# Moving the first two of four VectorE folds inside a top-k search: top-k attention followed by an expert layer

## The chip, the cores and the metric

The kernel runs on one core of one Trainium2 chip. The metric is the device time of one execution in microseconds. Engines are named as in the profile: PE is TensorE (PEld its weight loads), DVE is VectorE, ACT is ScalarE, POOL is GpSimd, SP is SyncE, which issues most of the DMAs.

## The reference

The first half is attention that keeps, for each query, the keys with the 32 highest scores. The second half routes each token to one of eight experts.

```python
# q, k, v: (8, 8, 576, 64) float32
scores = q @ k.T / sqrt(64)
kth = np.partition(scores, -32, axis=-1)[..., -32:-31]
scores = np.where(scores >= kth, scores, -1e9)
attn = softmax(scores)                      # + 1e-9 in the divisor
x = (attn @ v) as (8 * 576, 8 * 64)         # tokens x 512
logits = x @ w_gate                         # 8 experts
e = argmax(logits);  gate_w = softmax(logits)[e]
y = gate_w * (relu(x @ w1[e]) @ w2[e])      # 512 -> 1024 -> 512
```

## The kernel before

Work is cut into 144 items, here called slots: 8 batches of 18, each with two tiles of 128 queries against 576 keys. The list `work` holds them, and the function `loop` (L1123) goes through it. Its body writes out one order of instructions for TensorE, ScalarE and VectorE by hand (`tc.manual_schedule`, L1204), and these three engines run it as written. GpSimd's arithmetic keeps its program order too (`in_turn`). In one slot `i`:

- `products` (L292) has TensorE compute scores, and `scores` (L299) has ScalarE copy them from PSUM into a tile `s`. This runs three slots ahead (`AHEAD = 3`).
- `fold` and `fold_on` make the search shorter. With the 576 scores of a query as two halves, `fold` writes the larger of each pair to `h` (L306) and the smaller to `l` (L308). `fold_on` does the same with the halves of `h`: the larger go to `few` (L314), the smaller to `hl` (L316). All four are VectorE operations on two tiles in SBUF.
- `search` (L333) finds the 32nd highest value. It first takes the eight highest of `l` and of the two halves of `hl` into `few` (L345), and then does four rounds on `few`: a scan for the eight highest (L354), and, but for the last round, their replacement (L362), each for both tiles. After round 0 GpSimd computes `nbias` (L358).
- After the search, ScalarE scales the threshold to `low` (L371) and turns the scores into `w` (L387, `depths`); GpSimd subtracts `w` from `s` twice, once for each tile (L396, `less`), and computes `doubt` (L377); ScalarE takes the exponential (L404), TensorE transposes (L415 to L429), ScalarE copies the result out, and TensorE multiplies by the values (L450).

The search has places, called `tick`, after each scan and each replacement of rounds 1 to 3, where one operation of another job may stand on VectorE. These jobs wait in the list `aside`. They are the reciprocal of the divisors `rz` (L479, once per unit of nine tiles, after ScalarE's L472 to L477); once per batch the choice of the expert (L510 to L520) and the places of the rows (L546 to L556); and in six batches the tables of blocks (L611 to L651, over two slots).

GpSimd has more in its queue: products with the divisors for the logits (L487 to L492) and for the rows `x` (L500), the indirect DMAs that scatter the rows (L567), and those that store the output (L808).

The expert blocks (L893, L910) are cut into pieces, and `loop` places a number of them in each slot that it works out from the slot's index. What is left of them after the last slot runs as a tail on TensorE.

The search is called with a function `then`, which stands in front of the last round's scans:

```python
for r in range(R):
    if r == R - 1:
        then()
    for m in m_all:
        nc.vector.max(out=tops[:, m, r * 8:(r + 1) * 8], in_=src[m])
        if r:
            tick()
```

Of the kernel before, what the change touches and what calls it, by code (L numbers as in the profile page):

```python
# [42 lines left out]
def kernel(  # L43
# [216 lines left out]
    def open_unit(n):  # L260
        n.z = k.small.tile([P, NT], F32, name="z")

    def tails(tiles):
        return tiles[0][1] == 2 * NC
# [30 lines left out]
    def scores(got):  # L295

        s = k.att.tile([P, 2, 2, HF], F32, name="s", bufs=2 if k.exact else 4)
        return s, [
            lambda m=m, ps=ps: nc.scalar.copy(s[:, m, :, :], ps[:, :, 0:HF]) for m, ps in enumerate(got)  # L299
        ]  # L300

    def fold(s):

        f = SimpleNamespace()
        f.h = k.att.tile([P, 2, HF], F32, name="h", bufs=1)
        nc.vector.tensor_tensor(f.h, s[:, :, 0, :], s[:, :, 1, :], op=ALU.max)  # L306
        f.l = k.att.tile([P, 2, HF], F32, name="l")
        nc.vector.tensor_tensor(f.l, s[:, :, 0, :], s[:, :, 1, :], op=ALU.min)  # L308
        return f

    def fold_on(f):

        f.few = k.att.tile([P, 2, LW], F32, name="few", bufs=3)
        nc.vector.tensor_tensor(f.few[:, :, 0:QF], f.h[:, :, 0:QF], f.h[:, :, QF:HF], op=ALU.max)  # L314
        f.hl = k.att.tile([P, 2, QF], F32, name="hl", bufs=1)
        nc.vector.tensor_tensor(f.hl, f.h[:, :, 0:QF], f.h[:, :, QF:HF], op=ALU.min)  # L316
# [66 lines left out]
    def depths(s, low):  # L383

        w = k.att.tile([P, 2, S], F32, name="w", bufs=1 if k.exact else 3)
        for m in range(2):
            nc.scalar.activation(  # L387
                w[:, m, :], s[:, m, :, :].rearrange("p j k -> p (j k)"), AF.Relu,
                scale=-STEEP, bias=low[:, m:m + 1],
            )  # L390
        return w

    def less(s, w):

        for m in range(2):
            k.last_pool = in_turn(nc.gpsimd.tensor_tensor(  # L396
                w[:, m, :], s[:, m, :, :].rearrange("p j k -> p (j k)"), w[:, m, :], op=ALU.subtract
            )).ins
# [403 lines left out]
    def evacuate(upto=None):  # L802

        while due and (upto is None or upto in [kind for kind, _ in due]):
            due.pop(0)[1]()
# [131 lines left out]
    with fast:  # L937
# [30 lines left out]
        def put_stores():  # L968
            while stores:
                stores.pop(0)()  # L970
# [6 lines left out]
        def pieces(n):  # L977
            nonlocal current, left
            while n > 0 and left > 0:
                if current is None:  # L980
                    if not landed(loaded[0]):
                        break
                    now = loaded.pop(0)
                    if hasattr(now, "half"):
                        current = long_block(now, following)
                    else:
                        current = block(now, following, stores.append)
                    ahead()
                if clock is None:
                    evacuate()  # L990
                step = next(current)
                if step == "pause":
                    if clock is not None:
                        break
                    continue
                if step == "last":
                    current = None
                n -= 1
                left -= 1
            return n  # L1000

        def scatter(n):
            nonlocal left
            for _ in range(min(n, len(scatters))):
                scatters.pop(0)()
            if not scatters and coming:
                waiting.extend(coming)
                left += len(coming) * PIECES
                coming.clear()
                ahead()  # L1010
# [88 lines left out]
        def at_place(name):  # L1099
            for end in list(late):  # L1100
                if end[1] == name:
                    end[1] = next(end[0], None)
                    if end[1] is None:
                        late.remove(end)

        got_of, s_of, f_of, w_of = {}, {}, {}, {}

        def tiles_of(i):
            b, g = work[i]
            return [(unit[b * U + u], tile) for u, tile in g]  # L1110

        def turning(i):
            return transposed(tiles_of(i), w_of.pop(i))

        def multiply(i):
            tiles = tiles_of(i)
            got_of[i] = products(tiles)
            n, tile = tiles[0]
            more = n.b * U + n.u + 2
            if tile == (NC - 1 if n.u % 2 else 2 * NC) and more < len(units):  # L1120
                unit.append(load_unit(*units[more]))

        def loop():  # L1123
            nonlocal credit, rate, clock
            for i in range(min(AHEAD, len(work))):
                multiply(i)
                s_of[i], steps = scores(got_of.pop(i))
                for step in steps:
                    step()
            multiply(AHEAD)  # L1130
            f_of[0] = fold(s_of[0])
            fold_on(f_of[0])
            for i, (b, g) in enumerate(work):
                tiles = tiles_of(i)
                u, tile = g[0]
                if tile == 0 and u % 2 == 0:
                    open_unit(tiles[0][0])
                if tails(tiles):
                    open_unit(tiles[1][0])

                then = lambda: None
                if i + 1 < len(work):
                    f_of[i + 1] = fold(s_of[i + 1])
                    then = lambda: fold_on(f_of[i + 1])
                low, nbias, doubts = search(tiles, s_of[i], f_of.pop(i), then)
                at_place("small")
                w_of[i] = depths(s_of[i], low)
                less(s_of.pop(i), w_of[i])
                doubts()
                put_stores()  # L1150
                scatter(1)
                at_place("pool")
                at_place("relu")
                at_place("rows")
                at = i % per_batch
                if at == FIRST and b:
                    rate = new_of[b - 1] * PIECES / (U * NT)
                credit += rate * len(g)
                room = left
                if b == B - 1 and at >= ARRIVED:  # L1160
                    room -= KEEP
                    credit = room / (len(work) - i)
                share = {0: 0.5, 1: 1.2, 2: 1.6, 3: 0.5, 2 * NC: 1.4}[tile]
                now = max(0, min(int(credit * share + 0.5), room))
                credit -= now
                clock = i
                if i + AHEAD < len(work):
                    s_of[i + AHEAD], steps = scores(got_of.pop(i + AHEAD))
                    for step in steps:
                        step()  # L1170
                evacuate()
                at_place("turn")
                turns = turning(i - 1) if i else iter(())
                next(turns, None)
                part = min(BETWEEN, now - now // 2)
                rest = pieces(part)
                next(turns, None)
                rest = pieces(now - now // 2 - part + rest)
                weights(tiles, w_of[i], nbias)
                next(turns, None)  # L1180
                evacuate()
                if i + AHEAD + 1 < len(work):
                    multiply(i + AHEAD + 1)
                if tile == NC - 1:
                    end = ending(b, u)
                    late.append([end, next(end)])
                at_place("products")
                at_place("weights")
                credit = min(credit + pieces(now // 2 + rest), 6 * rate)

            for _ in turning(len(work) - 1):
                pass
            assert len(late) == 1
            clock = None
            for place in late[0][0]:
                if place == "rows":
                    pieces(4)
            kept = left - (SURE + HALVES + PLAIN) * PIECES
            assert kept >= 0, kept
            k.apart = True  # L1200
            pieces(kept)

        credit = rate = 0.0
        with tc.manual_schedule(engines={mybir.EngineType.PE, mybir.EngineType.Activation, mybir.EngineType.DVE}):  # L1204
            loop()
# [132 lines left out]
```

## Time and profile before

| | |
|---|---|
| time, median of 3 runs | 1338.02 us (1337.96 to 1338.56) |
| the profiled execution | 1339.03 us |
| its span, first to last instruction | 1337.4 us |
| mean granted TensorE clock | 0.955 |
| busy: PE, DVE, ACT, POOL | 1189.3, 1076.6, 930.8, 661.9 us |
| HBM read, written | 191.42 MB, 21.80 MB |

The page divides the span into 40 slices and gives each engine's busy share in tenths. A group line gives line, engine, operation, tiles and count, then the busy time in us and the mean of one instruction in ns, then the idle time before them and what ended it. A timeline line gives start, duration, engine, line, operation and count; instructions of one kind in a row are merged. A waits line names who waited for whom: total us, times, longest.

### The profile page before, as it was taken

The numbers are of one execution on the slowest core, as the hardware profiler recorded it, in microseconds if no ns is written. First come the engines' busy times: TensorE is split into PE (matmuls) and PEld (weight loads), VectorE is DVE, ScalarE is ACT, GpSimd is POOL, SyncE is SP. The second block draws the span as 40 slices with busy tenths as digits, with TensorE's granted clock in tenths as the row PEclk, the third lists the DMA queues.
The fourth block names the chain that finished last, engine by engine and source line by source line (L and its number), as shares of the span: only waits on it lengthen the run. The fifth ranks groups of instructions, "written<-read, shape, count | busy, mean of one in ns | idle before, by whom it ended". The sixth has DMA issues, their size and how long they took to land. (4 is left out here: it accounts for less than half of the span.)

```text
span 1337.4 us, 24295 instructions
## 1 busy us (share of the span) xinstructions
PE 1189.3 (89%) x7570; PEld 831.4 (62%) x7570; DVE 1076.6 (81%) x4629; ACT 930.8 (70%) x2125; POOL 661.9 (49%) x805
## 2 busy tenths in 40 slices
PE   5667766766799999999999999999999999999995
PEld 3344443444466766676677666666677667699973
DVE  7999999999999999999999999999999932000000
ACT  4788788887888888888787888887778851111110
POOL 3454547555755665567555756475547642000000
PEclk9788788888899999999999999999999999999998
DMA  2000001001384348435855294329452739946790
GB/s 84 30 29 30 30 29 65 29 29 38 122 305 168 108 164 288 160 110 175 297 208 179 74 350 170 118 76 372 171 204 87 283 116 332 369 146 219 290 342 18
DMA packets 95563, 214.36 MB, mean 160 GB/s; under 512 B 4926, under 2 KB 25662, under 8 KB 95424
## 3 DMA queue, kind: packets, MB, share of 16 engines
q1 hardware_dynamic: 88800, 192.45, 40.8%
q0 software_dynamic: 6336, 19.97, 4.2%
q8 instruction: 61, 1.00, 0.3%
q14 instruction: 78, 0.64, 0.2%
q10 hardware_dynamic: 288, 0.30, 0.1%
HBM read 191.42 MB, written 21.80 MB: 159 GB/s over the span
## 5 line engine op out<-in xcount | busy, mean ns | idle before, releaser
L396 POOL TENSOR_TENSOR w<-s,w 128x576 f32<-128x576 f32 x288 | 410.2, 1444 | 418.4 <-ACT w L387 418.4
L893 PE MATMUL ph<-xTs,w 128*128 128x128 f32 x2048 | 250.2, 276 | 5.9 <-ACT xTs L790 5.9
L893 PEld LDWEIGHTS ph<-xTs,w 128*128 128x128 f32 x2048 | 239.1, 192 | 21.9 <-issue 14.6
L910 PE MATMUL py<-w,hT 128*128 128x512 f32 x512 | 236.2, 597 | 0.0
L404 ACT ACTIVATE w<-w,nbias 128x576 f32<-128x576 f32 x288 | 224.1, 792 | 3.0 <-POOL w L396 2.0
L292 PE MATMUL sc<-qkb 64*128 64x288 f32 (+1 forms) x1280 | 206.0, 473 | 9.5 <-ACT s L299 5.1
L387 ACT ACTIVATE w<-s,low 128x576 f32<-128x576 f32 x288 | 207.6, 768 | 4.7
L415 PE MATMUL wTm<-turn,w 128*128 128x128 f32 x1152 | 170.1, 287 | 32.0 <-ACT xl L468 21.4
L415 PEld LDWEIGHTS wTm<-turn,w 128*128 128x128 f32 x1152 | 132.0, 145 | 92.5 <-issue 34.4
L299 ACT COPY s<-sc 128x576 f32<-128x576 f32 x288 | 168.9, 640 | 10.4 <-PE sc L292 10.4
L1217 DVE CAST any_i<-pd 1x1 int32<-1x1 f32 x1 | 0.1, 145 | 207.9 <-PE pd L1215 207.9
L422 ACT COPY wT<-wTm 128x512 f32<-128x512 f32 x256 | 139.2, 604 | 39.3 <-PE wTm L415 39.2
L354 DVE MAX8 tops<-scr 128x8 f32<-128x168 f32 x576 | 162.8, 317 | 0.0
L450 PE MATMUL po<-wT,vb 128*64 128x288 f32 x1024 | 154.9, 450 | 0.4 <-ACT wTt L437 0.4
L354 DVE MAX8 tops<-few 128x8 f32<-128x144 f32 (+1 forms) x576 | 154.4, 300 | 0.0
L292 PEld LDWEIGHTS sc<-qkb 64*128 64x128 f32 (+1 forms) x1280 | 110.1, 195 | 65.4 <-issue 25.6
L910 PEld LDWEIGHTS py<-w,hT 128*128 128x128 f32 x512 | 90.7, 190 | 90.4 <-issue 89.2
L808 POOL DMA_INDIRECT out_dram<-y,xg x40 | 42.6, 1066 | 189.8 <-ACT y L869 82.5
L345 DVE MAX8 few<-l 128x8 f32<-128x288 f32 x288 | 127.3, 442 | 0.0
L450 PEld LDWEIGHTS po<-wT,vb 128*64 128x64 f32 x1024 | 74.2, 150 | 77.3 <-issue 26.0
L306 DVE TENSOR_TENSOR h<-s 128x576 f32<-128x576 f32 x144 | 114.8, 797 | 3.9 <-ACT s L299 3.7
L308 DVE TENSOR_TENSOR l<-s 128x576 f32<-128x576 f32 x144 | 108.0, 750 | 0.0
(175 smaller groups left out, 1649.8 us busy)
## 6 DMA issues: line engine op xcount, KB each, us to landing
w<-in_moe_w_dram SPq DMA_DIRECT2D x72, 2048.0 KB, 8.6
qkb<-in_qk_dram SPq DMA_DIRECT2D x31, 608.0 KB, 5.8
vb<-in_v_dram SPq DMA_DIRECT2D x32, 320.0 KB, 3.1
xg<-x_rows SPq DMA_DIRECT2D x36, 257.0 KB, 10.6
x_rows<-blank SPq DMA_DIRECT2D x5, 257.0 KB
x_rows<-blank POOLq DMA_DIRECT2D x4, 257.0 KB, 8.2
x_rows<-x,posi POOLq DMA_INDIRECT x40, 3.1
out_dram<-y,xg POOLq DMA_INDIRECT x40, 4.5
```

Of the source, the lines that this page charges most:

```text
L292: nc.tensor.matmul(ps[rows, j, 0:HF], n.q[d, cols], n.k[d, keys], start=True, stop=True)
L299: lambda m=m, ps=ps: nc.scalar.copy(s[:, m, :, :], ps[:, :, 0:HF]) for m, ps in enumerate(got)
L345: nc.vector.max(out=f.few[:, m, QF + 8 * j:QF + 8 * j + 8], in_=away)
L354: nc.vector.max(out=tops[:, m, r * 8:(r + 1) * 8], in_=src[m])
L387: nc.scalar.activation(w[:, m, :], s[:, m, :, :].rearrange("p j k -> p (j k)"), AF.Relu, scale=-STEEP, bias=low[:, m:m + 1],)
L396: k.last_pool = in_turn(nc.gpsimd.tensor_tensor(w[:, m, :], s[:, m, :, :].rearrange("p j k -> p (j k)"), w[:, m, :], op=ALU.subtract)).ins
L404: nc.scalar.activation(w[:, m, :], w[:, m, :], AF.Exp, scale=scale, bias=nbias[:, m:m + 1], accum_out=n.z[:, c:c + 1])
L415: nc.tensor.transpose(pm[:, c * P:(c + 1) * P], w[:, m, first:first + P], ident)
L422: nc.scalar.copy(wT[:, :, m, q], pm4)
L450: nc.tensor.matmul(po[r, 0:HF], n.v[:, c, r], rhs, start=(c == 0), stop=(c == KC - 1))
L893: nc.tensor.matmul(ph[:, f, :], n.w1[:, 0, dt, fc * P:(fc + 1) * P], n.xT[:, dt, :], start=(dt == 0), stop=(dt == DT - 1),)
L910: nc.tensor.matmul(py, hT[:, f, :], n.w2[:, 0, f, :], start=(f == 0), stop=(f == FT - 1))
```

## The change

Before, `loop` issued the next slot's `fold` (`h` and `l`) ahead of the call of `search`, and handed it `fold_on` (`few` and `hl`) as `then`. Now `then` holds both, so that all four folds of the next slot stand together in front of the last round's scans. Nothing else differs; the first slot's folds stand ahead of the loop as before.

```diff
                 then = lambda: None
                 if i + 1 < len(work):
-                    f_of[i + 1] = fold(s_of[i + 1])
-                    then = lambda: fold_on(f_of[i + 1])
+                    def then():
+                        f_of[i + 1] = fold(s_of[i + 1])
+                        fold_on(f_of[i + 1])
                 low, nbias, doubts = search(tiles, s_of[i], f_of.pop(i), then)
```

## The prediction

> **What bounds the kernel now.** I read the page's busy times and slices first, then VectorE's groups by form, then what VectorE waits for, then the timeline of single slots. A slot here is the time from one `h` fold of L306 to the next.
>
> ```profile
> PE 1189.3 (89%) x7570; PEld 831.4 (62%) x7570; DVE 1076.6 (81%) x4629; ACT 930.8 (70%) x2125; POOL 661.9 (49%) x805
> ...
> PE   5667766766799999999999999999999999999995
> ...
> DVE  7999999999999999999999999999999932000000
> ...
> PEclk9788788888899999999999999999999999999998
> ```
>
> VectorE is full from the second slice to about 1066 us, where the last search ends; TensorE is a third idle for the first 11 slices and full only after some 400 us. The last 270 us are TensorE's alone. Each slot carries a fixed share of the expert blocks, so time added to a slot is added to the span, unless TensorE and ScalarE set that slot's pace. In the waits of 50 to 300 us, ScalarE's `low` waits 29.2 us in 29 slots for the search; in those of 650 to 750 us it never does. So VectorE sets the pace early, TensorE and ScalarE between about 645 and 815 us and again from about 920 us.
>
> The groups by form give the folds:
>
> ```profile
> L306 DVE TENSOR_TENSOR h<-s 128x576 f32<-128x576 f32 x144 | 114.8, 797 | 3.9 <-ACT s L299 3.7
> L308 DVE TENSOR_TENSOR l<-s 128x576 f32<-128x576 f32 x144 | 108.0, 750 | 0.0
> ...
> L314 DVE TENSOR_TENSOR few<-h 128x288 f32<-128x288 f32 x144 | 78.4, 544 | 0.0
> L316 DVE TENSOR_TENSOR hl<-h 128x288 f32<-128x288 f32 x144 | 71.6, 497 | 0.0
> ```
>
> An undisturbed slot shows 0.74, 0.75, 0.45 and 0.45 us for the four, so the means hide a few long ones. A plain slot on VectorE, on GpSimd, and the end of ScalarE's divisor chain in it:
>
> ```profile
> 273.55 0.74 DVE L306 TENSOR_TENSOR h<-s 128x576 f32<-128x576 f32 x1
> 274.21 0.75 DVE L308 TENSOR_TENSOR l<-s 128x576 f32<-128x576 f32 x1
> ...
> 277.35 0.20 DVE L479 RECIPROCAL rz<-rz 128x10 f32<-128x10 f32 x1
> ...
> 279.33 0.45 DVE L314 TENSOR_TENSOR few<-h 128x288 f32<-128x288 f32 x1
> 279.69 0.45 DVE L316 TENSOR_TENSOR hl<-h 128x288 f32<-128x288 f32 x1
> 280.06 0.56 DVE L354 MAX8 tops<-scr 128x8 f32<-128x168 f32 x2
> 280.54 0.74 DVE L306 TENSOR_TENSOR h<-s 128x576 f32<-128x576 f32 x1
> ```
> ```profile
> 274.76 2.84 POOL L396 TENSOR_TENSOR w<-s,w 128x576 f32<-128x576 f32 x2 [3.77 <-ACT w L387]
> 277.56 0.20 POOL L377 TENSOR_TENSOR doubt<-few,tops 128x6 f32<-128x6 f32 x1
> 277.73 0.21 POOL L358 TENSOR_SCALAR nbias<-tops 128x2 f32<-128x2 f32 x1
> ```
> ```profile
> 276.41 0.20 ACT L475 ACTIVATE rz<-z 64x1 f32<-64x1 f32 x1
> ```
>
> Counted from the slot's `h`: GpSimd's two subtractions run from 1.21 to 4.05, the side steps that `tick` lets in begin at 3.80, the second pair of folds stands at 5.78. A slot with nothing else lasts 6.92 us; the mean over the loop is 7.4. What happens when a VectorE instruction on two SBUF operands, or a small cast or shift, meets a GpSimd subtraction:
>
> ```profile
> 450.54 1.21 DVE L613 TENSOR_SCALAR ci<-ci 1x8 int32<-1x8 int32 x1
> ```
> ```profile
> 448.93 2.79 POOL L396 TENSOR_TENSOR w<-s,w 128x576 f32<-128x576 f32 x2 [3.96 <-ACT w L387]
> ```
>
> A 1x8 shift takes 1.21 us instead of the 0.17 of another slot, and ends as the subtraction ends: one waits for the other, whole. The scans, replacements and reciprocals show no such growth under the subtractions.
>
> **What moves.** No instruction is added or removed; the DMAs are untouched, and GpSimd's arithmetic keeps its program order. `h` and `l` leave the head of the search and stand with `few` and `hl` ahead of the last two scans. The last scan of a search has the same work in front of it as before, so `low`, and with it the subtractions, keep their place: 0.1 and 1.21 us after the end of the previous search. The inputs of `h` were copied by ScalarE two slots before, so moving it later can add no wait (four waits of 3.7 us in all can only go). What lies between the two places comes earlier by the starts of `h` and `l`, 0.66 + 0.67 = 1.33 us: the eight scans and the replacements, and with them every `tick`. The first one falls at 2.47 instead of 3.80, into the middle of the subtractions instead of onto their end. The fold block spans 4.37 to 6.44.
>
> **Divisors.** The reciprocal of L479 waits for ScalarE's `rz`; the 12.1 and 1.6 us in VectorE's waits are ten cases of it. Behind a waiting reciprocal stands the rest of the search, so `low` and everything after it wait too. I took the end of the last `rz` from the slot's start in the 24 slots where the reciprocal is the first side step. Four end before 2.2: no cost. Four at 2.50: 0.05 each. Five between 3.0 and 3.3: 3.6 us together. Eleven end at 3.75 or later and pay the full 1.33: 14.6. Sum +18.4 us, from 0 if ScalarE moved forward too, which nothing in the change makes it do.
>
> **Choice, places and tables.** In 7 + 7 + 12 slots the ticks let in chains of small operations. Five choice slots have the `oh` comparison (L512) at 2.81 with a subtraction running to 4.0 or beyond: 1.05 each, by the shift's 1.21 - 0.17; the other two have their subtractions after 6.1. Eight of the twelve table slots pay about 1.0 more than now (L613 and L642 are the ones that stop); four have late subtractions and trade one stop for another. The places chain meets them at L552: 0.4 twice, 0.8 three times, 1.2 twice. Sum 5.3 + 8.0 + 5.2 = +18.5. Bounds 0 and 26 x 1.4, one whole subtraction each.
>
> **The fold block.** Laid over GpSimd's lines, slot by slot. Now the four folds lose 31 us in 46 long instances. Relieved: eight `h` that stand behind `rows` (L500), 0.59 each, -4.7; four `h` behind late subtractions or late copies, -4.1. New: in some fifteen slots the second subtraction ends after 4.5 and `h` waits for it, 5.1 together; ten where `doubt` ends just after 4.4, 1.5; five where a subtraction ends at 4.65, 1.2; a dozen where a logits step (L489, 0.27 alone) slips in between two folds, 3; and slots as at 511 to 534 us, where the subtractions end at 6.0 to 6.5: now one fold waits 0.2 to 0.6, then two would, 1.5 to 1.75, +3.6 in each of two such groups. The nine with `rows` over `few` stay at about 0.6. Sum +10. Lower bound -31, all losses of now gone. Upper bound +35: in some 23 slots GpSimd's `lg` or `rows` arrives during the block, and if it gets in between any two folds, these pay one `rows` (1.26) nearly whole, 1.1 each or 25 more. I take +10, as the block covers 2.07 us of a place that GpSimd's late work reaches, where the pair covered 0.74.
>
> Here a rule speaks against the change. At 360.62 us GpSimd's `rows` takes 2.49 us instead of 1.26: it waited for `h` and `l` both. So an undisturbed pair holds GpSimd off, and my +10 rests on that. The Trainium skill (SBUF — State Buffer, "SBUF: two separate sides") says that the port shared by the two engines is locked for one whole instruction and that whoever starts first has it; read strictly, GpSimd would enter after each fold and the block would pay as in the upper bound, which would put the sum at +59 instead of +34.
>
> **The sum.** 18.4 + 18.5 + 10 = 47 us. About 13 of them (seven of the eleven full divisor waits, 9.3; the rest two places slots and one group of late subtractions, less the relieved `h`) lie where TensorE and ScalarE set the pace, and I take these as hidden by them; without that cover they count. So +33 to +34 us. The profiled execution took 1339.03 us with a span of 1337.4; its median of the runs is 1338.02. +33 on the median: 1371 us.
>
> **Rivals.** The measurement can tell about 0.2%, 2.7 us, from no change.
> - Faster: with no two-operand instruction in the first 4.37 us of a slot, GpSimd runs free there, is done before the block and the 31 us of fold losses go. For it: the plain slot, where `nbias` ends at 4.39, just at the block. It decides once the relief exceeds the side steps' cost; with the relief whole, the divisors paid only outside TensorE's stretches (9) and the small steps' cost halved (9), the time is 1338 - 31 + 18 = 1325. Against it: in 69 of 144 slots `doubt`, which follows the subtractions, starts later than 4.4. 7%.
> - No difference: the order of a full engine's own work doesn't matter, or the order on the chip isn't that of the source, though L1204 fixes it for VectorE; 1338, 4%. Against it: `low` waits on the search in 60 slots.
> - TensorE hides more: only the first 400 us (54 slots) count, divisors 5, small steps 5, folds 0: 1348. 5%.
> - Much slower: GpSimd alternates with the four folds wherever it arrives, the upper bound above: 1338 + 18 + 19 + 35 - 13 = 1397; it decides if `h` and `l` no longer hold GpSimd off as a pair. 16%.
> - Forecast: 1371, on its own 1355 to 1385. 68%.
>
> **How the numbers follow.** Faster 0.07, within 0.2% 0.05, slower 0.88. The range reaches down to the case of more cover and up into the alternating one: 1346 to 1396.
>
> **What would show it.** `RECIPROCAL rz` should wait some 25 to 32 us for ScalarE instead of 13.7; the small steps L512, L613, L642, L552 should have means well above now, with GpSimd's L396 running over them; L306 should take over the long instances from L314; slots without side steps should still last 6.92 us. It is wrong if those slots lengthen, if the reciprocal's waits don't grow, or if the mean of the four folds falls to 0.74, 0.75, 0.45, 0.45.

## The result, and the profile after

The changed kernel takes 1353.60 us (median; 1351.78 to 1354.69), the kernel before in the same runs 1337.99: +15.6 us, a ratio of 1.0114 with a 95% interval of 1.0101 to 1.0128. It is slower, as forecast, and inside the range, but by less than half of the +33 us of the forecast. The profiled execution took 1351.78 us, its span 1350.2, 12.8 more than before.

VectorE's groups by form (busy us, mean ns, then idle before them and its cause); first three of the kernel before:

```profile
L479 DVE RECIPROCAL rz<-rz 128x10 f32<-128x10 f32 x32 | 6.5, 202 | 13.7 <-ACT rz L475 12.1 <-ACT rz L477 1.6
...
L514 DVE TENSOR_TENSOR oh<-oh,e_less 128x40 f32<-128x40 f32 x8 | 1.5, 185 | 0.0
...
L637 DVE SCALAR_TENSOR_TENSOR slot_f<-slot_f,done,slots 1x5 f32<-1x5 f32 x2 | 0.5, 255 | 0.0
```

The changed kernel:

```profile
L306 DVE TENSOR_TENSOR h<-s 128x576 f32<-128x576 f32 x144 | 121.0, 841 | 1.6 <-ACT s L299 1.6
L308 DVE TENSOR_TENSOR l<-s 128x576 f32<-128x576 f32 x144 | 118.0, 820 | 0.0
...
L314 DVE TENSOR_TENSOR few<-h 128x288 f32<-128x288 f32 x144 | 65.5, 455 | 0.0
L316 DVE TENSOR_TENSOR hl<-h 128x288 f32<-128x288 f32 x144 | 65.4, 454 | 0.0
...
L479 DVE RECIPROCAL rz<-rz 128x10 f32<-128x10 f32 x32 | 6.8, 212 | 20.6 <-ACT rz L475 17.5 <-ACT rz L477 3.1
L514 DVE TENSOR_TENSOR oh<-oh,e_less 128x40 f32<-128x40 f32 x8 | 6.2, 776 | 0.0
...
L552 DVE TENSOR_SCALAR den<-den 128x5 f32<-128x5 f32 x8 | 4.1, 517 | 0.0
L647 DVE TENSOR_SCALAR upto_all<-upto_all 1x9 f32<-1x9 f32 x7 | 3.5, 503 | 0.0
...
L637 DVE SCALAR_TENSOR_TENSOR slot_f<-slot_f,done,slots 1x5 f32<-1x5 f32 x2 | 2.9, 1429 | 0.0
```

The four folds together are busy 369.9 us instead of 372.8: `few` and `hl` have become clean, `h` and `l` carry the losses. The reciprocal waits 20.6 us instead of 13.7. Small operations stop: L514 has a mean of 776 ns (185 before), L552 517 (322), L647 503 (156), and the 1x5 form of L637 1429 (255).

Put side by side slot by slot, from the end of one search to the end of the next, the two traces account for nearly all of it. The last search ends 13.3 us later, 10.3 us of which are there by slot 87. Inside the loop, summed over what each instruction takes beyond its undisturbed length (0.74, 0.75, 0.45 and 0.45 us for the folds, 0.17 for a small step; a fold counts from 0.1 us beyond it, a small step from 0.07):

| us lost in the loop | before | after | difference | forecast |
|---|---|---|---|---|
| reciprocal waiting for ScalarE | 7.6 | 14.3 | +6.7 | +18.4 |
| small steps stopped | 11.5 | 23.7 | +12.2 | +18.5 |
| folds stopped | 30.8 | 25.8 | -5.0 | +10 |
| hidden by TensorE and ScalarE | | | none left to subtract | -13 |
| sum | | | +13.9 | +33 to +34 |

The 1.9 us that `h` waited for ScalarE's copies are gone besides, which leaves 1.3 us of the 13.3 in differences too small for this count.

A slot without side steps that nothing disturbs lasts 6.92 us in both. The change is a balance of slots that grow and slots that shrink: choice slots 22 and 40 last 8.47 instead of 7.56 us, table slots 44, 62, 80 and 116 8.7 instead of 7.5, since L637 takes 1.42 us there under a subtraction; the nine slots in which `rows` lay over `few` last 6.92 instead of 7.5 (once 7.9).

ScalarE waits for the search more often, before and then after:

```profile
ACT low L371 <- DVE tops L354: 63.0, 60, 4.1
```
```profile
ACT low L371 <- DVE tops L354: 95.1, 87, 3.7
```

What becomes of GpSimd's `rows` when it meets the block of four is seen in the timeline of slot 44 (not one of the nine), GpSimd first, then VectorE:

```profile
332.10 3.40 POOL L500 TENSOR_TENSOR x<-xl,rz 128x640 f32<-128x640 f32 x1
```
```profile
332.23 0.74 DVE L306 TENSOR_TENSOR h<-s 128x576 f32<-128x576 f32 x1
332.90 0.74 DVE L308 TENSOR_TENSOR l<-s 128x576 f32<-128x576 f32 x1
333.56 0.44 DVE L314 TENSOR_TENSOR few<-h 128x288 f32<-128x288 f32 x1
333.93 0.44 DVE L316 TENSOR_TENSOR hl<-h 128x288 f32<-128x288 f32 x1
```

`rows` takes 1.26 us alone. It waited until the last of the four folds had read, 2.14 us, and VectorE lost nothing. In slot 12, one of the nine, a logits step that takes 0.27 us elsewhere waits in the same way:

```profile
98.81 2.14 POOL L489 TENSOR_TENSOR lg<-lg,xl 128x40 f32<-128x40 f32 x1
```

### The profile page after: what moved, and what is told of

Same layout as the page of the kernel before. It is cut to its first block, busy times and chain, and to the rows that moved or that the text cites. A ratio compares the mean times of both kernels' runs of the same rounds, so it can differ in the third digit from the quotient of the medians.

```text
span 1350.2 us, 24292 instructions
## 1 busy us (share of the span) xinstructions
PE 1197.9 (89%) x7570; PEld 836.4 (62%) x7570; DVE 1085.3 (80%) x4629; ACT 932.0 (69%) x2125; POOL 727.1 (54%) x805
## 5 line engine op out<-in xcount | busy, mean ns | idle before, releaser
L396 POOL TENSOR_TENSOR w<-s,w 128x576 f32<-128x576 f32 x288 | 415.1, 1463 | 370.2 <-ACT w L387 369.5
L415 PE MATMUL wTm<-turn,w 128*128 128x128 f32 x1152 | 173.8, 292 | 37.1 <-ACT xl L468 26.6
L415 PEld LDWEIGHTS wTm<-turn,w 128*128 128x128 f32 x1152 | 135.3, 148 | 97.5 <-issue 34.6
L450 PE MATMUL po<-wT,vb 128*64 128x288 f32 x1024 | 157.0, 455 | 0.4 <-ACT wTt L437 0.4
L808 POOL DMA_INDIRECT out_dram<-y,xg x40 | 49.6, 1240 | 189.8 <-ACT y L869 82.4
L450 PEld LDWEIGHTS po<-wT,vb 128*64 128x64 f32 x1024 | 75.1, 152 | 78.2 <-issue 27.7
L306 DVE TENSOR_TENSOR h<-s 128x576 f32<-128x576 f32 x144 | 121.0, 841 | 1.6 <-ACT s L299 1.6
L308 DVE TENSOR_TENSOR l<-s 128x576 f32<-128x576 f32 x144 | 118.0, 820 | 0.0
```

The costliest lines, as they stand in the source:

```text
L396: k.last_pool = in_turn(nc.gpsimd.tensor_tensor(w[:, m, :], s[:, m, :, :].rearrange("p j k -> p (j k)"), w[:, m, :], op=ALU.subtract)).ins
L415: nc.tensor.transpose(pm[:, c * P:(c + 1) * P], w[:, m, first:first + P], ident)
L450: nc.tensor.matmul(po[r, 0:HF], n.v[:, c, r], rhs, start=(c == 0), stop=(c == KC - 1))
```

## Experiments: are the side steps to blame?

The theory: the loss comes from the side steps' new place, 1.33 us earlier, where they meet the subtractions and ScalarE's unfinished divisors; the fold block itself gains. The main rival: the block, or the later start of the folds, costs the time.

**Side steps back, folds together.** In the changed kernel, ticks only from round 2 on:

```diff
                 nc.vector.max(out=tops[:, m, r * 8:(r + 1) * 8], in_=src[m])
-                if r:
+                if r > 1:
                     tick()
+                if r == R - 1:
+                    tick()
...
-                    if r:
+                    if r > 1:
                         tick()
```

> The changed kernel, but side steps stand on VectorE only from round 2 of a search on (two at each of the last scans, so that as many fit). The first then falls 3.56 us after the previous search's end instead of 2.47, near the 3.80 of the kernel before; the four folds stay together. Theory (the loss is the side steps' new place: divisors +7, small steps +12, folds -5 us): about 1335 us, reciprocal waits of 15 us or less, L514, L647, L649 back below 0.3 us. Rival (the fold block, or the later start of the folds, costs the time and the side steps are innocent): 1350 to 1355 us.

Measured 1341.90 us, ratio to before 1.0023 (1.0014 to 1.0032). 11.7 of the 15.6 us are gone with the folds left where the change put them. The rival falls, though the 1335 us of the theory are missed by 7. The reciprocal waits 2.4 us in the loop; L514 (there the line of the comparison that is L512 above) and the tables still stop, 21.4 us in all. Six of these stops, 0.87 us each, come at the end of the tables, which now run into a third slot.

**Folds back, side steps early.** In the kernel before, `if r:` is taken away from both ticks, so that they begin in round 0.

> The kernel before, folds where they were, but side steps let in from round 0 on: the first falls 2.83 us after the previous search's end instead of 3.80. Theory: the loss comes without moving any fold, 1345 to 1354 us (small steps +8 to +12, divisor waits 18 to 20 us instead of 13.7, the fold losses of before unchanged). Rival (fold block): 1338 us.

1352.56 us, 1.0104 (1.0089 to 1.0119): without moving a fold, nearly the whole loss. VectorE's waits show it:

```profile
DVE rz L477 <- ACT rz L473: 22.7, 13, 6.1
...
DVE rz L477 <- ACT rz L475: 5.5, 6, 1.8
```

28.2 us instead of 13.7, and the small steps lose 22.6 instead of 11.5 us in the loop. The make-up differs from the changed kernel's: the reciprocal's wait in the loop grows by 14.5 us, twice as much as there, and the folds lose 22.1 us instead of 30.8, although none was moved. So the run shows that earlier side steps cost this much without a moved fold; that its total is so near the changed kernel's is partly chance.

**One kind at a time.** In the changed kernel, a tick before round 2 does nothing while the reciprocal stands first in `aside` in one run, while anything else stands first in the other (both with a second tick at the last scans):

```diff
+            if r < 2 and aside[0] in divs:      # the other run: not in divs
+                return
             if next(aside[0], "end") != "end":
```

> The changed kernel, but only the divisors' reciprocal has to wait for round 2; choice, places and tables come as in the changed kernel. Theory: the divisor term alone goes, 7 us: about 1347 us, small steps as slow as in the changed kernel. Rival (what I had forecast for the divisors, 18 us): 1335 us. Rival (fold block): 1353 us.

> The changed kernel, but choice, places and tables wait for round 2; only the reciprocal comes as in the changed kernel. Theory: the small steps' term goes, 12 us: about 1341.5 us, reciprocal waits still about 20 us. Rival (fold block): 1353 us.

1349.02 us (1.0082, 1.0068 to 1.0096) and 1345.00 us (1.0061, 1.0047 to 1.0074): the divisors are worth 4.6 us, the small steps 8.6, together 13.2, about what both together brought. My forecast of 18 us for the divisors is refuted, and each term is about two thirds of what I now expected. In the trace of the second, the reciprocal still waited 11.5 us in the loop, against 14.3. In the trace of the first its wait did not simply go: it fell from 5.8 to 1.4 us in the first 87 slots, where the folds lost 7.5 us instead of 4.9, and rose from 1.8 to 5.6 us in each of slots 91 and 127. The 4.6 us are what was left of such exchanges in the medians; the two profiled executions lie only 1.4 us apart.

**What is left.** To see whether the tables' third slot explains the 3.6 us above the kernel before, all side steps went into round 2, two at each place, so that ten fit.

> The changed kernel, all side steps in round 2, two at each place, one after each of the last scans. Ten fit in a slot, so that no table spills into a third slot as it does in the run with steps from round 2 on (stops of 0.87 us there, in six slots). Theory: that run's 1341.9 us less 4 to 6, 1335.5 to 1338 us, level with the kernel before or a little under. Rival (what is left above the kernel before is the fold block in the stretch that TensorE paces): 1341 to 1343 us.

1340.31 us, 1.0014 (1.0005 to 1.0023): between the two. The small steps' loss falls from 21.4 to 15.8 us, and 1.7 us are left against the kernel before. In that trace the folds lose 32.3 us against 30.8, all of the excess behind slot 87: in the stretch that TensorE paces, the block's relief doesn't show.

## Experiments: when do folds and subtractions stop each other?

**The block among the subtractions.** In the changed kernel, `if r == R - 1: then()` becomes `if r == 1: then()`.

> The changed kernel, but the four folds stand in front of round 1, where GpSimd's two subtractions run (2.23 us after the previous search's end). Theory: h waits 0.3 us for the first subtraction, the second then gets in before l, which waits 1.2: 1.5 us in each plain slot, 1440 to 1480 us in all. Rival (once h runs the four hold GpSimd off): h waits 0.3 in each, less the side steps' cost: about 1355 us.

1506.62 us, 1.1255 (1.1234 to 1.1275), more than I expected. The means by form, and one plain slot on VectorE and GpSimd:

```profile
L308 DVE TENSOR_TENSOR l<-s 128x576 f32<-128x576 f32 x144 | 273.4, 1899 | 0.0
```
```profile
61.53 1.01 DVE L306 TENSOR_TENSOR h<-s 128x576 f32<-128x576 f32 x1
62.47 1.95 DVE L308 TENSOR_TENSOR l<-s 128x576 f32<-128x576 f32 x1
64.34 0.45 DVE L314 TENSOR_TENSOR few<-h 128x288 f32<-128x288 f32 x1
```
```profile
60.52 3.28 POOL L396 TENSOR_TENSOR w<-s,w 128x576 f32<-128x576 f32 x2 [4.05 <-ACT w L387]
```

Here the two alternate: `h` waits 0.27 us for the first subtraction, the second gets in ahead of `l`, and `l` waits 1.2. So two patterns stand side by side. A run of folds that begins undisturbed mostly keeps GpSimd out until its end; a fold that had to wait first lets the next GpSimd operation in behind it. Where a block of four stands decides which of the two it meets.

The changed kernel's trace shows how far this goes. In all 22 blocks that GpSimd's arithmetic came upon and whose `h` had to wait, it got in before the block's end. Of the 52 such blocks that began undisturbed, 37 kept it out to the end. In the other 15, among them slots 27 and 60, an indirect DMA of GpSimd was running as `h` began, and the operation behind it got in after `h` or `l`; in slot 27 `nbias` (0.21 us alone) ends as `l` does, with `few` and `hl` still to come:

```profile
207.03 0.50 POOL L358 TENSOR_SCALAR nbias<-tops 128x2 f32<-128x2 f32 x1
```

Seven of the 37 had such a DMA over their beginning too; what tells the two apart was not tested.

The Trainium skill (SBUF — State Buffer, "SBUF: two separate sides") has the port held for one whole instruction by whoever starts first; the alternation agrees with that, while slot 44 above shows it held over four.

**A gap in the block.** In the changed kernel, the last scan of tile 0 moves between `l` and `few`:

```diff
             if r == R - 1:
-                then()
+                then(0)                    # h, l
             for m in m_all:
+                if r == R - 1 and m:
+                    then(1)                # few, hl
                 nc.vector.max(out=tops[:, m, r * 8:(r + 1) * 8], in_=src[m])
```

> The changed kernel, but with the last scan of tile 0 between the pair h, l and the pair few, hl. Theory (GpSimd is held off by folds that follow each other without a gap, four of them in the changed kernel): a logits step gets in after l, and rows behind it meets few again, in some 25 slots: 3 to 10 us slower than the changed kernel, 1357 to 1363 us, and L314's mean rises above 0.50 us. Rival (each instruction holds the port by itself, so that the order alone changes nothing): 1353.6 us, L314 at 0.455.

1361.52 us, 1.0174 (1.0160 to 1.0188): 7.9 slower than the changed kernel. Slot 44 again, now on GpSimd and VectorE (L502 is the line of `rows` here):

```profile
334.14 2.66 POOL L502 TENSOR_TENSOR x<-xl,rz 128x640 f32<-128x640 f32 x1
```
```profile
334.94 0.74 DVE L308 TENSOR_TENSOR l<-s 128x576 f32<-128x576 f32 x1
335.85 1.26 DVE L314 TENSOR_TENSOR few<-h 128x288 f32<-128x288 f32 x1
```

In the gap `rows` gets in, after 1.40 us of waiting instead of 2.14, and `few` pays 0.81. So in this slot it is the gapless run that keeps GpSimd out. But L314's mean is 487 ns, below the 500 that I had expected: the folds lose 27.7 us in the loop against 25.8, and 6.2 of the 7.9 us are the reciprocal's, which I had not expected. The time is as forecast for a reason that is only partly the one given; the next section but one comes back to it.

## Experiments: can the side steps be placed better?

**All four folds at the head of the search**, the opposite move, with `hl` given a second buffer and `scr` laid into the used-up `l`:

```diff
                     f_of[i + 1] = fold(s_of[i + 1])
-                    then = lambda: fold_on(f_of[i + 1])
+                    fold_on(f_of[i + 1])
```

> The opposite move: all four folds of the next slot stand at the head of a search (hl gets a second buffer and scr lies in the used-up l tile to make room). Side steps then begin 4.54 us after the previous search's end. Theory: the folds, back to back, hold the subtractions off until 2.07 (0.86 us later, which ScalarE's exponential has to spare), divisor waits fall from 13.7 to about 4 us, fold losses from 31 to about 10: 1315 to 1330 us, and the two kernels of this case are both beaten. Rival (the later subtractions put off the exponential and the chain behind it): 1338 to 1350 us.

1361.46 us, 1.0167 (1.0148 to 1.0186): wrong, and worse than the rival's number too. In eleven slots `nbias` or `rows` reaches into the head, `h` waits for it, and then both subtractions get in; here in slot 22:

```profile
168.49 0.85 DVE L306 TENSOR_TENSOR h<-s 128x576 f32<-128x576 f32 x1
169.26 0.74 DVE L308 TENSOR_TENSOR l<-s 128x576 f32<-128x576 f32 x1
169.93 1.65 DVE L314 TENSOR_TENSOR few<-h 128x288 f32<-128x288 f32 x1
171.50 1.67 DVE L316 TENSOR_TENSOR hl<-h 128x288 f32<-128x288 f32 x1
```

`h` loses 0.11, `few` and `hl` 1.2 each. The folds lose 27.5 us in the first 87 slots (9.3 before). The forecast had taken the undisturbed pattern for granted.

**Later side steps in the kernel before**: ticks from round 2 in one run, only the reciprocal put off in the other.

> The kernel before, side steps only from round 2 on (first at 4.89 us instead of 3.80), two at each of the last scans. Theory (side steps cost by what GpSimd and ScalarE do at that time): divisor waits fall to about 4 us where VectorE sets the pace, the small steps of three table slots (1 us each) go: 1329 to 1334 us. Rival (side steps were already clear of the subtractions, later ones gain nothing): 1338 us.

> The kernel before, only the divisors' reciprocal put off to round 2 (4.89 us after the previous search's end instead of 3.80). Theory: the 7.6 us that it waits inside the loop go where VectorE sets the pace (1 us) and move VectorE closer to ScalarE elsewhere: 1331 to 1337 us. Rival (behind 640 us VectorE is held by the subtractions, so that what the reciprocal saves is waited for by a fold): 1337 to 1339 us.

1337.43 us (0.9990, 0.9981 to 0.9999) and 1338.02 us (0.9994, 0.9985 to 1.0003): nothing that is worth having. In both, the reciprocal's wait in the loop falls from 7.6 to 1.4 us, yet the last search ends no earlier (1078.6 and 1079.2 us, against 1077.8 and 1079.9 in the two traces of the kernel before). Put off alone, the reciprocal's 6.2 us come back as fold losses (35.4 against 30.8) and as waits of `h` for ScalarE's copies (4.1 against 1.9). That wait was slack that stood somewhere.

**All side steps behind the block**, four after each of the last two scans, none elsewhere:

> The changed kernel, side steps only behind the four folds, four after each of the last two scans (as many as fit in two slots). Theory: no side step meets the subtractions where VectorE sets the pace, the reciprocal never waits there, and the folds keep their relief of some 5 us: 1329 to 1336 us, better than both kernels; small steps over 0.24 us lose less than 2 us in the first 88 slots. Rival (what is taken out of the middle comes back at the end, as GpSimd's rows wait behind the folds just there): 1338 to 1343 us.

1346.64 us, 1.0056 (1.0042 to 1.0070); the theory's number is missed, and the rival's too. The small steps lose 2.0 us in the first 87 slots (3.5 in the kernel before) and the reciprocal nothing, but the folds lose 12.8 there (9.3 in the kernel before, 4.9 in the changed one): in table slots 61 and 79 the subtractions, which ran from 2.5 to 5.3 us after the search's end in the kernel before, run from 4.0 to 7.3, and `h` and `l` stop for 2.0 us over them. Why ScalarE comes later to these slots was not followed, nor why the last search ends 4.3 us later than before in this trace and the program 7.7.

No order that was tried beats the kernel before by more than the measurement can tell.

## Why the divisors cost less than forecast

> The changed kernel unaltered, for a second trace. Theory (the divisors wait for ScalarE, which waits for TensorE, whose granted clock dips differ from run to run): fold and small-step losses as in the first trace within 1 us, the reciprocal's wait different by 1 to 5 us and the time with it. Rival (all terms are fixed by the order): the same to 0.5 us in each.

> The kernel before unaltered, for a second trace. Theory: its first side step has 1.33 us more to spare, so that a dip of the clock reaches the reciprocal seldom: its wait within 1 us of 13.7. Rival: it varies as much as in the changed kernel.

One execution each: 1353.43 and 1339.91 us. The second trace of the changed kernel has 23.7 us for small steps, the same, 26.8 for folds (25.8) and 21.0 us of reciprocal waits (20.6). Neither text is quite right: the sum hardly moves, but single slots do. Slot 37 waits 1.27 us in one trace and not at all in the other, slot 46 0.50 and 1.46. In the kernel before, the sum is 14.1 us against 13.7.

The reciprocal waits for ScalarE, which waits for TensorE's product L450. TensorE ahead of slot 64, in the kernel before and in the changed one:

```profile
468.21 2.16 PE L450 MATMUL po<-wT,vb 128*64 128x288 f32 x16
```
```profile
475.16 3.67 PE L450 MATMUL po<-wT,vb 128*64 128x288 f32 x16
```

The granted clock over the second was 0.59, and 1.00 over the same product one slot later. The reciprocal then waited 1.13 us; in the run with the scan between the folds, with such a dip in the same place (0.50 between 478 and 482 us), 2.41 us. So those 6.2 us of that run came at least partly through the clock. That the kernel before, with its first side step at 3.80 us, had slack for more of such dips than the changed kernel at 2.47 fits this, and is argued, not tested. Why the clock dips at different slots in different runs was not pursued.

In the stretch that TensorE paces another thing happens. In slots 91, 105, 109, 127 and 141 the reciprocal waits as long as before (1.78 us in slot 91, 1.77 after). There a fold waits for the end of a late subtraction, and that fixes VectorE's place against ScalarE. Before it was `few`, with 1.25 us of work to the end of the search, now it is `h`, with 1.33 more. The search ends 1.33 us later against ScalarE, and the first tick, 1.33 us nearer to that end, falls where it fell.

## Right and wrong, step by step

- **Bound, removed and added work**: right. VectorE sets the pace, a plain slot stays at 6.92 us, the subtractions keep their place there (1.13 us after the search's end in both). The last search ends at 1077.8 us, though, not at about 1066.
- **The mechanism**: right. Side steps that move by 1.33 us run into the subtractions and the divisors; two runs show it from both sides.
- **The fold block, +10 us: the step that failed.** Measured -5.0 (-4.4 of it in the first 87 slots), so 15 of the some 20 us that the forecast was too high. (Its parts as listed add up to +9.2.) Three of its parts are wrong. "The nine with `rows` over `few` stay at about 0.6": all nine went to nothing, 4.9 us in the first 87 slots alone, since the gapless four keep the logits steps and `rows` out there. "Some fifteen slots" with `h` behind a late second subtraction: slots 68, 69, 77, 86 and 87 show no such wait, where the second subtraction now ends 3.9 to 4.7 us after the search's end instead of 4.5 to 5.1. The stops put in elsewhere had delayed VectorE, and ScalarE and GpSimd were less late; ScalarE's `low` waits 87 times for the search now, 95.1 us, against 60 times and 63.0. I had laid the new order over the old lateness. And a group as at 511 to 534 us pays 1.8 us instead of the 4.9 that its three slots were to pay. The upper bound needed what the run with the scan between shows in part; the paragraph on 2.49 us for `rows` behind `h` and `l` had the right rule, and I applied it to two folds where it holds for four.
- **The small steps, +18.5 us**: 12.2. Five slots (61, 79, 115; 76, 112) already had a stop of 0.8 to 1.0 us. It moved, and cost 0.16 to 0.21 more instead of a whole second one. Places cost 0.25 to 0.3 in each of their seven slots, not 0.4 to 1.2 (the forecast's seven add up to 5.6, not to 5.2). L613 stopped as forecast; beside it L514 stopped instead of L512, and L637 in slots 44, 62, 80 and 116 instead of L642, 1.17 us more each; in slots 98 and 134 L647 and L649 took over a stop that L637 had before.
- **The divisors, +18.4 us, half of it hidden**: 6.7 against some 9. The seven in TensorE's stretch were hidden, as taken, but for 0.73 each in slots 100 and 136. Of the four full waits before slot 87, three did not grow: "from 0 if ScalarE moved forward too, which nothing in the change makes it do" was the wrong side to lean on.
- **The rivals**: the faster one had the sign of the fold term right; its price of 31 us was six times too high, since the losses behind slot 87 only changed places (`few` and `hl` to `h` and `l`). GpSimd's subtractions alternated with the block in eight slots behind slot 87 (89, 90, 95, 103, 125, 126, 131, 139), where late subtractions had met the folds before as well, and in no slot whose subtractions were on time.

## What to carry to other kernels

Moving work on a full in-order engine moves everything between its two places as well: list what those instructions meet on the other engines at their new time, before weighing what the moved ones gain. Waits read off an old trace don't simply add to a new one: a stop put in early takes away lateness, and with it later stops, so a slot-by-slot overlay over-counts. A wait that disappears without a change in time was slack; put off, it comes back on the next instruction.

## What the runs showed of the hardware

Four VectorE operations on two SBUF operands each, issued without a gap, kept GpSimd's arithmetic out for all of their 2.1 us in 37 of the 52 undisturbed blocks above, and in slot 44 one scan in between let it in. They held up some of GpSimd's indirect DMAs too. Here one (L567) takes 3.00 us with a block of folds over it, where another (L808) shortly before takes 1.04, as both do alone in the loop:

```profile
480.85 1.04 POOL L808 DMA_INDIRECT out_dram<-y,xg  x1 [0.15 <-issue]
482.20 3.00 POOL L567 DMA_INDIRECT x_rows<-x,posi  x1 [0.30 <-issue]
```

In the changed kernel's trace the twelve that lie under a whole block take 2.8 to 3.2 us; others take the usual 1.04 with `h` and part of `l` over them, as the one in slot 27 at 205.97 us.

A 1x8 shift on VectorE can be stopped by a 1.4 us subtraction of GpSimd until it takes seven times its own length (1.21 us instead of 0.17; a 1x8 cast took 1.27 in the run with all side steps in round 2), while scans of 168 elements over the same subtraction lose nothing.
